# Reordering six items' steps in a hand-planned attention and MLP kernel: one transpose-back and one normalisation earlier, one score product ahead of a value product, two filler steps out

## The chip, the cores and the metric

The kernel runs on 1 core of one Trainium2 chip. The metric is the device time of one execution in microseconds. A core has five engines that each work through a list of their own in order: TensorE (PE, with its weight loads shown apart as PEld), VectorE (DVE), ScalarE (ACT), GpSimd (POOL) and SyncE (SP, which here only issues DMAs). They wait for one another by semaphores.

## The reference

Eight batches of twelve heads, 448 positions, 64 features, go through attention with normalised queries and keys; the result, seen as 3584 tokens of 768 features, goes through an MLP with a hard swish.

```python
q_n = q / (np.linalg.norm(q, axis=-1, keepdims=True) + 1e-06)
k_n = k / (np.linalg.norm(k, axis=-1, keepdims=True) + 1e-06)
scores = np.matmul(q_n, k_n.transpose(0, 1, 3, 2)) / tau
scores = scores - np.max(scores, axis=-1, keepdims=True)
attn = np.exp(scores)
attn = attn / (np.sum(attn, axis=-1, keepdims=True) + 1e-09)
out = np.matmul(attn, v)
...
h = x @ w_in                     # 768 -> 2048
g = h * np.clip(h + 3.0, 0.0, 6.0) / 6.0
return g @ w_out                 # 2048 -> 768
```

## The kernel before, in words

**Items.** The work of the attention is cut into 48 items, numbered from 0; an item is two heads of one batch (A and B), six items make a batch. Items 0 to 5 are batch 0, item 6 is the first of batch 1. The change calls them first, second and so on: the second item is number 1, the fourth 3, the fifth 4, the sixth 5, the seventh 6.

**An order written out by hand.** `PLAN` (lines 19 to 117) is a long list of steps such as `SC.5.3.1`. A loop at the end (line 1198) runs through it and calls for each step the function of that name with its numbers; each issues its instructions on its engine there and then. So the order of the list is the order of each engine's own list, and two steps on different engines only order each other where one needs the other's data or buffer. The framework puts the semaphore waits in. A letter at the end of a step names the engine (v for DVE, p for POOL, a for ACT).

**The steps of an item.** `LQ` and `LV` load queries, keys and values (SP, lines 254 to 281). `SQ`, `RE` and `NO` make the norms (any engine, DVE, ACT). `NM.j` scales a pair of items' queries or keys with them (line 333; j counts such pairs: items 6 and 7 are pairs 6 and 7). `TR.j` transposes them on PE into one of two PSUM banks, Y or Z (line 393), and copies bring the parts to SBUF: `CQ.i` the queries of item i (line 431), `CK.i` its keys (line 436), and from item 6 on `CS.i` the last 64 keys of either head, apart (line 450: for items 6 and 7 a memset and two small copies on DVE). `kz0` holds the keys of even items, `kz1` of odd ones.

`SC.i.g` makes the scores of item i on PE, keys along the partitions (line 474). Group g of 0, 1, 2 is a block of 128 keys of head A and one of head B, as two matmuls into two banks; group 3 is what is left of both, 64 keys each. `EX.i.g` takes exp on ACT, from PSUM to SBUF (line 508). No maximum is subtracted. `VA.i.g` multiplies the exps with the values on PE, 8 small matmuls of 65 columns for each block, all into the one accumulator PV (line 529); the 65th column is the sum of the exps. `VC.i` brings the values into bf16 (line 352).

`FI.i` is the normalisation of an item's result (line 548): a reciprocal of the sums and a multiplication, both on DVE, from PV to an SBUF tile `on`. PV is free for the next item's first `VA` once `FI` has read it. There are two buffers of `on`, and each holds two items: items 0 and 1, then 2 and 3, then 4 and 5 in the buffer of 0 and 1:

```python
        if i % 2 == 0:
            needs(("BK", i - 4), ("BK", i - 3))
            twin_on[i // 2] = sb.tile([128, 2, 4, 2, D], BF16, name="on", tag="on", bufs=2)
```

`BK.i` transposes an item's `on` on PE into a bank (four transposes, line 565), and `CX.i` copies it into `xT`, the input of the MLP (line 585). Later items go through a crossbar DMA instead (`XB`, `XP`; and `XD` in place of `TR`, line 404).

**Banks.** In the start-up phase, items 0 to 5, scores go to two tiles of two banks each (`SC0`, `SC1`; the last number of `SC.5.3.1` names the tile), and Y and Z serve the transposes. `OPEN` (line 1146) ends this phase: the four banks become M0 to M3, and from then on scores, transposes and MLP products take their banks in turn from one ring:

```python
        ring.extend([m[0], m[1], Y, Z, m[2], m[3]])
```

So `SC.6.0`, the first after `OPEN`, goes to M0 and M1, `SC.6.1` to Y and Z, `BK.4` to M2, `SC.6.2` to M3 and M0, and so on. With `startup.close()` the old tiles are given back, and the new ones wait for the readers of the old.

**Fillers.** `DP.n` issues n matmuls of 248 columns on zeros, into a part of PV that nobody reads (line 1139):

```python
            nc.tensor.matmul(
                PV[:, 0, 260:508], zeros[:, 0:128], zeros[:, 0:248], start=first, stop=first, skip_group_check=True
            )
```

**The MLP.** `F.b.n` is a 128-feature block of the first product (six matmuls of 448 columns, line 662), `FA` and `FV` its hard swish on ACT and DVE; `G`, `P`, `PE` and others make the second product with sums that save multiplications. From 39 us on these steps stand between those of the attention; the last two batches' first product follows the attention.

Of the kernel before, what the change touches and what calls it, by code (L numbers as in the profile page):

```python
# [23 lines left out]
    "TR.3.Y CK.2.v SC.1.3.1 DP.1 SC.2.0.0 SQ.6.a.0.7 VA.1.0 VA.1.2 EX.1.3 SC.2.1.1 NM.5.p RE.7 EX.2.0 EX.2.1 CK.3.v VA.1.3 RE.6 SQ.8.p.0.7 VA.1.1 SC.2.2.0",  # L24
    "FI.1 EX.2.2 SC.2.3.1 EX.2.3 TR.4.Y VA.2.0 NO.3 LV.2 CQ.3.v SC.3.0.0 CQ.4.v CQ.5.v VC.4.v VA.2.1 VA.2.2 VA.2.3 SC.3.1.1 FI.2 TR.5.Z EX.3.0 EX.3.1",
    "CK.4.v BK.0.Y LV.3 LQ.9 RE.8 SC.3.2.0 SC.3.3.1 VA.3.0 EX.3.2 SC.4.0.0 EX.3.3 EX.4.0 CK.5.v CX.0.v SQ.9.v.0.7 VA.3.2 SC.4.1.1 VA.3.1 SC.4.2.0 VA.3.3",
    "FI.3 BK.2.Z CX.2.v EX.4.1 EX.4.2 NM.6.p TR.6.Y SC.4.3.1 EX.4.3 SC.5.0.0 EX.5.0 VA.4.0 RE.9 W.3 W.1 VA.4.3 SC.5.1.1 VC.6.p VA.4.2 VA.4.1 CQ.7.v CQ.6.v",
    "SC.5.2.0 EX.5.1 EX.5.2 NM.7.p TR.7.Z CK.6.v VC.5.p LQ.10 BK.3.Y CX.3.v SQ.10.p.0.7 SC.5.3.1 CS.7.v EX.5.3 NO.4 BK.1.Y FI.4 DP.3 VA.5.0 CS.6.v OPEN",
    "VA.5.2 SC.6.0 CX.1.v CK.7.v NM.8.p EX.6.0 VA.5.3 VA.5.1 FI.5 SC.6.1 EX.6.1 BK.4 CX.4.v SC.6.2 SC.6.3 EX.6.2 EX.6.3 BK.5 CX.5.v VA.6.0 VA.6.1 TR.8",
    "CQ.8.v CQ.9.v LQ.11 SQ.11.p.0.7 SC.7.0 VA.6.2 EX.7.0 VA.6.3 SC.7.1 SC.7.2 F.0.2 EX.7.1 EX.7.2 RE.11 RE.10 SC.7.3 EX.7.3 FA.0.2 F.0.7 FA.0.7 FI.6",  # L30
    "NM.9.p TR.9 CK.9.v CK.8.v CS.8.v CS.9.v F.0.1 LQ.14 LQ.13 SQ.13.a.0.7 NO.5 F.0.3 FA.0.1 FV.0.7 FV.0.2 FV.0.1 VC.7.p W.5 FA.0.3 LQ.12 LV.4 SQ.12.p.0.7",
    "SC.8.0 SC.8.1 FV.0.3 RE.12 LV.5 W.4 VC.8.p VA.7.0 EX.8.0 EX.8.1 NM.10.p F.0.0 FA.0.0 SC.8.2 VA.7.3 FV.0.0 VA.7.1 VA.7.2 VC.11.p EX.8.2 SC.8.3 EX.8.3",
    "SC.9.0 EX.9.0 F.0.4 RE.13 FI.7 SC.9.1 NM.11.p VC.10.p FA.0.4 FV.0.4 SC.9.2 TR.10 VA.8.0 VA.8.1 EX.9.1 NO.6 NM.13.p SC.9.3 CQ.11.v TR.11 CQ.10.v",
    "CS.11.v EX.9.2 EX.9.3 CK.11.v LQ.15 VA.8.2 F.0.6 VA.8.3 CS.10.v CK.10.v SC.10.0 FA.0.6 FV.0.6 EX.10.0 F.0.5 FA.0.5 SC.10.1 SC.10.2 SC.10.3 FI.8 VC.9.p",
    "VA.9.0 VA.9.2 VA.9.1 EX.10.1 EX.10.2 EX.10.3 FV.0.5 VA.9.3 FI.9 SC.11.0 EX.11.0 F.0.10 FA.0.10 FV.0.10 SQ.14.a.0.7 NM.12.p W.9 VA.10.0 TR.12 CQ.13.v",
    "CQ.12.v VA.10.1 SC.11.1 VA.10.3 SC.11.2 XP.6 VA.10.2 FI.10 EX.11.1 EX.11.2 F.0.14 FA.0.14 BK.8 SC.11.3 EX.11.3 CX.8.a BK.9 VA.11.0 TR.13 VA.11.2 RE.14",
    "CS.12.a CX.9.v LV.6 FV.0.14 CK.12.v CS.13.a CK.13.v F.0.15 FA.0.15 VC.12.p SQ.15.p.0.7 FV.0.15 SC.12.0 SC.12.1 RE.15 EX.12.0 EX.12.1 VA.11.1 F.0.13",
    "SC.12.2 VA.11.3 FI.11 FA.0.13 FV.0.13 BK.10 CX.10.a NO.7 F.0.12 FA.0.12 EX.12.2 F.0.9 W.8 LQ.16 SQ.16.v.6.1 SQ.16.p.0.6 RE.16 VA.12.0 BK.11 CX.11.v",
    "NM.15.p NM.14.p FV.0.12 F.0.8 LQ.20 LQ.17 LQ.19 SQ.17.a.0.7 RE.17 FA.0.8 SC.12.3 FV.0.8 G.6.0.p FA.0.9 FV.0.9 F.1.4 FA.1.4 EX.12.3 FV.1.4 F.1.1 FA.1.1",
    "FV.1.1 SC.13.0 SC.13.1 SQ.19.v.0.7 RE.19 EX.13.0 EX.13.1 LQ.18 SQ.18.p.0.7 F.1.5 FA.1.5 FV.1.5 LV.7 XD.15 XD.14 W.7 W.6 F.1.9 FA.1.9 FV.1.9 F.0.11",  # L40
    "VA.12.3 VC.13.a WS.7.1 FA.0.11 FV.0.11 F.1.15 FA.1.15 F.1.6 G.1.0.p G.2.0.p FA.1.6 RE.18 FV.1.15 CS.14.v FV.1.6 NO.8 NM.16.p F.1.8 SC.13.2 CK.15.v",
    "VA.12.1 LQ.21 SQ.21.p.0.7 VC.15.p SC.13.3 VA.12.2 FA.1.8 FV.1.8 FI.12 VC.14.a F.1.0 NM.17.v WS.y4.1 EX.13.2 EX.13.3 NO.9 F.1.10 CK.14.v FA.1.10",
    "FV.1.10 FA.1.0 NM.18.p GL.0.p FV.1.0 F.1.11 FA.1.11 SC.14.0 FV.1.11 EX.14.0 F.1.12 FA.1.12 FV.1.12 SC.14.1 SC.14.2 F.1.3 SQ.20.a.0.7 FA.1.3 G.7.0.v",
    "EX.14.1 EX.14.2 VA.13.0 VA.13.3 VA.13.2 VA.13.1 FI.13 FV.1.3 F.1.7 FA.1.7 FV.1.7 XD.16 SC.14.3 SC.15.0 VA.14.0 VA.14.2 VA.14.1 EX.14.3 EX.15.0 XD.17",
    "WS.6 SC.15.1 SC.15.2 VA.14.3 SC.15.3 EX.15.1 EX.15.2 F.1.2 FA.1.2 CK.16.v SC.16.0 EX.15.3 FI.14 CK.17.v FV.1.2 WS.y3 EX.16.0 LV.8 VC.16.a F.1.13",
    "FA.1.13 XP.12 LV.9 VA.15.0 VA.15.2 VA.15.3 SC.16.1 EX.16.1 SC.16.2 VA.15.1 NM.19.p CS.16.v XD.18 XD.19 FV.1.13 FI.15 F.1.14 FA.1.14 VC.17.a SC.16.3",
    "P.3.1 FV.1.14 LQ.22 XP.14 EX.16.2 WS.7.0 WS.y4.0 LQ.23 VA.16.0 SC.17.0 VA.16.1 G.5.0.p P.3.0 LV.11 RE.21 EX.16.3 VA.16.3 G.7.1.v EX.17.0 PE.3.1.a",
    "SC.17.1 SC.17.2 VA.16.2 CK.18.v PE.3.0.a EX.17.1 FI.16 XB.16 EX.17.2 P.5.0 PE.5.0.a SC.17.3 VA.17.0 RE.20 WS.1 VA.17.1 EX.17.3 SC.18.0 SC.18.1 EX.18.0",
    "EX.18.1 SC.18.2 VA.17.3 VA.17.2 G.5.1.p P.4.0 P.5.1.a FI.17 XB.17 NO.10 NM.20.v PE.4.0.v CK.19.v CS.18.v XD.20 LQ.24 LQ.25 VC.18.a P.1.0 P.7.0 EX.18.2",
    "BO.0 LV.10 SQ.22.a.0.7 G.1.1.p P.2.0 PE.2.0.a PE.1.0.v PE.7.0.v RS.0 SC.18.3 VA.18.0 NM.21.p XD.21 P.6.0 RE.22 PE.6.0.v SQ.23.a.0.7 RE.23 G.6.1.v",  # L50
    "LQ.26 VA.18.1 SC.19.0 EX.18.3 PE.5.1.a EX.19.0 VA.18.2 F.2.2 FA.2.2 FV.2.2 SQ.24.v.0.7 SC.19.1 SC.19.2 EX.19.1 EX.19.2 VA.18.3 FI.18 CK.21.v CK.20.v",
    "F.2.3 F.2.12 NO.11 FA.2.12 G.2.1.p FA.2.3 FV.2.3 NM.22.p LQ.27 PL.5.1 SC.19.3 FV.2.12 CS.20.v P.4.1 EX.19.3 XD.22 VC.19.v LV.12 F.2.13 FA.2.13 FV.2.13",
    "P.2.1.a F.2.14 VA.19.0 VA.19.2 F.2.5 NM.23.p LQ.28 XD.23 PE.2.1.a PE.4.1.v PL.2.1 VC.21.p BO.1 RS.1 SQ.25.a.0.7 F.2.11 VC.20.p RE.24 RE.25 VA.19.1",
    "FA.2.14 FV.2.14 FA.2.5 SQ.26.a.0.7 FA.2.11 F.2.6 FV.2.5 FV.2.11 VA.19.3 SC.20.0 SC.20.1 FA.2.6 FV.2.6 P.1.1 PE.1.1.v FI.19 EX.20.0 EX.20.1 SC.20.2",
    "VC.22.a NO.12 SC.20.3 F.2.9 CK.22.v FA.2.9 FV.2.9 EX.20.2 EX.20.3 P.6.1 PE.6.1.v F.2.7 XP.18 FA.2.7 FV.2.7 VA.20.0 VA.20.3 RE.26 SC.21.0 SC.21.1",
    "NM.24.v P.7.1 EX.21.0 LQ.29 LV.13 SC.21.2 SC.21.3 G.7.2.p NM.25.p VC.23.p EX.21.1 EX.21.2 VA.20.2 VA.20.1 G.6.2.p G.2.2.v PE.7.1.v SQ.27.a.0.7 RE.27",
    "F.2.8 CK.23.v CS.22.v XD.24 LQ.30 P.3.2 SC.22.0 VC.24.a EX.21.3 FA.2.8 FI.20 SQ.28.v.0.7 FV.2.8 RE.28 G.5.2.p PE.3.2.a EX.22.0 SQ.29.v.0.7 F.2.15",
    "FA.2.15 FV.2.15 NO.13 VA.21.0 P.5.2 PE.5.2.a VA.21.1 P.4.2 VA.21.3 PE.4.2.a BO.2 SC.22.1 SC.22.2 EX.22.1 EX.22.2 VA.21.2 RE.29 FI.21 XD.25 P.2.2",
    "PE.2.2.a SC.22.3 G.1.2.v NM.26.v VA.22.0 VA.22.1 SC.23.0 EX.22.3 SC.23.1 SC.23.2 VA.22.3 EX.23.0 EX.23.1 VA.22.2 CK.25.v FI.22 F.2.1 FA.2.1 SC.23.3",
    "FV.2.1 CK.24.v P.1.2 VA.23.0 F.2.4 XP.20 CS.24.v SQ.30.p.0.7 XD.26 PE.1.2.v NO.14 EX.23.2 EX.23.3 RS.2 NM.27.v LQ.32 LQ.31 P.6.2 VA.23.2 FA.2.4 FV.2.4",  # L60
    "SC.24.0 VA.23.3 PE.6.2.v SC.24.1 XD.27 SC.24.2 VA.23.1 EX.24.0 FI.23 P.3.3 NM.28.p NM.29.p EX.24.1 EX.24.2 SC.24.3 EX.24.3 PE.3.3.a XB.23 XB.22 P.7.2",
    "PE.7.2.v VC.25.p LQ.33 VA.24.0 VA.24.2 SC.25.0 SC.25.1 VC.26.a EX.25.0 SC.25.2 EX.25.1 VA.24.3 VA.24.1 EX.25.2 FI.24 G.1.3.v RE.30 F.2.10 SC.25.3",
    "EX.25.3 FA.2.10 CK.26.v FV.2.10 CK.27.v CS.26.v F.2.0 FA.2.0 FV.2.0 P.4.3 PE.4.3.a VA.25.0 VA.25.1 SC.26.0 SC.26.1 SC.26.2 VA.25.3 EX.26.0 VA.25.2",
    "G.7.3.v G.5.3.v G.6.3.v FI.25 EX.26.1 EX.26.2 SQ.32.a.0.7 SQ.31.p.0.7 F.3.11 F.3.12 FA.3.12 FA.3.11 P.5.3.a SC.26.3 EX.26.3 PE.5.3.a RE.31 G.7.4.v",
    "F.3.15 SQ.33.a.0.7 FA.3.15 NO.15 FV.3.11 G.5.4.v FV.3.12 G.2.3.p P.2.3.a VA.26.0 VA.26.2 XD.29 SC.27.0 SC.27.1 XD.28 CK.28.v FV.3.15 PE.2.3.v VA.26.3",
    "SC.27.2 LV.14 XP.24 LQ.34 LV.15 EX.27.0 EX.27.1 VA.26.1 FI.26 RE.33 PL.5.3 GL.2.p VC.27.v EX.27.2 F.3.0 FA.3.0 FV.3.0 F.3.3 FA.3.3 FV.3.3 F.3.14 F.3.4",
    "SC.27.3 RE.32 FA.3.14 VC.29.a NM.30.p LV.16 LQ.35 P.1.3 VA.27.0 VA.27.2 VA.27.1 FV.3.14 PL.2.3 EX.27.3 VA.27.3 SC.28.0 FA.3.4 BO.3 PE.1.3.v FV.3.4",
# [1167 lines left out]
```

## Time and profile before

| | |
|---|---|
| device time, three runs | 397.3, 398.22, 397.3 us (median 397.3) |
| the profiled execution | 397.24 us, of which the span of the instructions 395.4 |
| PE busy | 384.2 us, 97% of the span, 3782 matmuls |
| DVE busy | 308.8 us, 78% |
| ACT busy | 295.3 us, 75% |
| POOL busy | 297.5 us, 75% |
| HBM read, written | 46.73 MB, 11.01 MB |
| chain that ended last | PE 87%, POOL 5%, DVE 2%, DMA 2% |

How to read the views that follow. In a timeline a row has the start in us from the span's beginning, the duration of the row in us, the engine, the line of the kernel, the operation, what it writes and from what, how many instructions are merged in the row, and in brackets how long the engine stood idle before it and whose end released it. Matmuls are pipelined: the duration of a row goes to the end of the last one, so rows overlap; the step from one row's start to the next is what PE's list needs. In the busy time by stretches each row has the stretch, its length, and for PE, PEld, DVE, ACT and POOL the busy us and the number of instructions, then the granted clock, the share of the DMA engines' time, and GB/s. In the list of waits the numbers are the us in total, the count and the longest. Tile names have their numbers left out: `SC` is SC0 or SC1, `M` any of M0 to M3, `kz` either key tile, `PV` the accumulator.

### The profile page before, as it was taken

How to read it: one execution, taken by the hardware profiler on the slowest of the kernel's cores; microseconds unless marked ns; L12 is line 12 of the kernel's file. 1: busy time of each engine (PE TensorE's matmuls, PEld its weight loads, DVE VectorE, ACT ScalarE, POOL GpSimd, SP SyncE). 2: the span in 40 equal slices, each digit the busy share in tenths (PEclk: the TensorE clock that was granted, in tenths of full speed). 3: DMA queues.
4: the chain of work that ended last, by engine and by line, in shares of the span. 5: the costliest groups of instructions: out<-in, count | busy, mean ns of one | idle time of the engine just before them, and what ended most of it. 6: DMA issues, size and time to landing. Idle time of an engine off the chain costs nothing.

```text
span 395.4 us, 10013 instructions
## 1 busy us (share of the span) xinstructions
PE 384.2 (97%) x3782; PEld 240.4 (61%) x3782; DVE 308.8 (78%) x545; ACT 295.3 (75%) x670; POOL 297.5 (75%) x269
## 2 busy tenths in 40 slices
PE   7898999999999999999999999999999999999995
PEld 5565556445655555655655556655566679977763
DVE  6998869988969697787767878853878968986862
ACT  6997999889966888887757876897787567744420
POOL 4999894899589947477848684778798988675752
PEclk9999999999999999999999999999999999999999
DMA  8989989798999797886995599665456350012124
GB/s 294 327 225 279 201 248 259 135 173 166 225 206 235 161 233 191 167 211 194 174 222 136 151 200 183 193 150 133 105 124 139 80 117 2 2 41 61 41 60 119
DMA packets 90239, 64.87 MB, mean 164 GB/s; under 512 B 55760, under 2 KB 89424, under 8 KB 90192
## 3 DMA queue, kind: packets, MB, share of 16 engines
q1 hardware_dynamic: 85280, 57.56, 59.1%
q0 software_dynamic: 4512, 6.29, 9.5%
q8 instruction: 29, 0.48, 0.5%
q10 hardware_dynamic: 400, 0.39, 0.3%
q14 instruction: 18, 0.15, 0.1%
HBM read 46.73 MB, written 11.01 MB: 146 GB/s over the span
## 4 chain that ended last, share of the span: by engine, by line
PE 87%; POOL 5%; DVE 2%; DMA 2%; issue 2%; ACT 1%; SPq 0%; POOLq 0%; DVEq 0%; ACTq 0%
PE M L671 18%; PE M L837 17%; PE PV L537 10%; PE V L837 6%; PE M L1026 6%; PE M L502 6%; PE Y L671 4%; PE Y L837 4%; PE Z L837 4%; PE Z L671 3%; POOL nrm L341 2%; PE Y L502 2%; PE Z L502 2%; POOL vx L363 1%; PE Y L1026 1%
## 5 line engine op out<-in xcount | busy, mean ns | idle before, releaser
L521 ACT ACTIVATE att<-M 128x448 bf16<-128x448 f32 x193 | 95.7, 561 | 13.9 <-PE M L502 12.2
L671 PE MATMUL M<-xT,w_in_sb 128*128 128x448 bf16 x396 | 82.9, 353 | 0.0
L671 PEld LDWEIGHTS <-w_in_sb 128*128 128x128 bf16 x576 | 53.1, 98 | 46.8 <-issue 3.4
L341 POOL TENSOR_TENSOR nrm<-big,r 128x896 bf16<-128x896 f32 (+1 forms) x36 | 61.7, 1720 | 15.0 <-ACT r L329 13.8
L537 PEld LDWEIGHTS <-att 128*128 128x128 bf16 (+1 forms) x1536 | 55.5, 97 | 23.0 <-issue 10.4
L537 PE MATMUL PV<-vx,att 128*128 128x65 bf16 (+1 forms) x1536 | 64.1, 193 | 0.5 <-POOL vx L363 0.5
L837 PEld LDWEIGHTS <-gT 128*128 128x128 bf16 x448 | 43.0, 98 | 27.7 <-issue 0.4
L686 DVE SCALAR_TENSOR_TENSOR gT<-u,M 128x448 bf16<-128x448 bf16 x66 | 39.5, 616 | 18.7 <-ACT u L680 18.4
L310 DVE TENSOR_REDUCE n<-big 128x14 f32<-128x896 f32 (+1 forms) x50 | 51.5, 1042 | 1.6 <-ACT big L296 1.3
L680 ACT ACTIVATE u<-M 128x448 bf16<-128x448 f32 x66 | 35.8, 555 | 10.8 <-PE M L671 9.7
L298 POOL TENSOR_TENSOR big<-big 128x896 f32<-128x896 f32 (+2 forms) x19 | 31.5, 1658 | 12.4 <-DMA big<-in_k_dram 6.9
L837 PE MATMUL M<-w_out_sb,gT 128*128 128x384 bf16 x224 | 40.4, 326 | 0.0
L837 PEld LDWEIGHTS <-gs 128*128 128x128 bf16 x296 | 28.1, 98 | 18.8 <-issue 1.3
L812 POOL TENSOR_TENSOR gT<-gT 128x1024 bf16<-128x1024 bf16 x15 | 31.9, 2125 | 9.5 <-DVE gs L812 9.0
L558 DVE TENSOR_TENSOR on<-PV,rc 128x512 bf16<-128x512 f32 x48 | 33.2, 691 | 1.6
L837 PE MATMUL M<-w_sum,gs 128*128 128x384 bf16 (+1 forms) x192 | 34.0, 323 | 0.0
L502 PE MATMUL M<-tT,kz 64*128 64x448 bf16 (+1 forms) x171 | 33.2, 354 | 0.6 <-DVE gT L686 0.4
L868 POOL TENSOR_TENSOR big<-big 128x384 f32<-128x384 f32 x14 | 18.3, 1308 | 17.7 <-ACT big L625 15.0
L812 POOL TENSOR_TENSOR gs<-gT 128x1024 bf16<-128x1024 bf16 x14 | 29.7, 2126 | 2.3 <-DVE gT L686 1.2
L521 ACT ACTIVATE att<-Z 128x448 bf16<-128x448 f32 x51 | 28.5, 559 | 1.3 <-PE M L502 1.0
L521 ACT ACTIVATE att<-Y 128x448 bf16<-128x448 f32 x50 | 28.0, 561 | 1.2 <-PE Z L502 1.2
L458 POOL COPY km<-tT 64x128 bf16<-64x128 bf16 x34 | 16.4, 483 | 12.5 <-PE Y L502 5.1
(146 smaller groups left out, 756.6 us busy)
## 6 DMA issues: line engine op xcount, KB each, us to landing
big<-in_q_dram SPq DMA_DIRECT2D x24, 448.0 KB, 4.4
big<-in_k_dram SPq DMA_DIRECT2D x24, 448.0 KB, 4.5
out_dram<-o SPq DMA_DIRECT2D x107, 96.0 KB, 2.2
big<-in_v_dram SPq DMA_DIRECT2D x68, 128.0 KB, 3.2
big<-in_v_dram SPq DMA_DIRECT2D x7, 448.0 KB, 7.6
w_out_sb<-in_moe_w_out_dram POOLq DMA_DIRECT2D x4, 768.0 KB, 10.2
w_in_sb<-in_moe_w_in_dram POOLq DMA_DIRECT2D x4, 384.0 KB, 5.8
w_in_sb<-in_moe_w_in_dram POOLq DMA_DIRECT2D x2, 768.0 KB, 8.3
```

The source lines that it names most:

```text
L298: engines[e].tensor_tensor(out=o, in0=i, in1=i, op=ALU.mult)
L310: nc.vector.tensor_reduce(out=n2s[d % 2][:, j % 2, c], in_=sq[:, :, :, :].rearrange("p g c d -> p (g c) d")[:, c, :], axis=AX.X, op=ALU.add,)
L341: engines[e].tensor_tensor(out=nrm[:, :, g, :].rearrange("p c g d -> p g c d"), in0=raw_of[j][:, g, :, :], in1=rs[d % 2][3][:, j % 2, :] . ...
L502: nc.tensor.matmul(o, ks, qt[rows], start=True, stop=True)
L521: nc.scalar.activation(out=o, in_=x, func=AF.Exp, scale=inv_tau)
L537: nc.tensor.matmul(pv_out(j, h), at[rows, n, q_cols(i // HP, j)], vt[rows, 3 + h if name == "M" else 5 * h + int(name[1]), :], start=(name ...
L558: nc.vector.tensor_tensor(out=on[:, :, :, :].rearrange("p j h d -> p h j d"), in0=pv4[:, :, :, 0:D], in1=rc[:, :, :].to_broadcast([128, 2, ...
L671: nc.tensor.matmul(ps[:, 0:S], w_in_sb[:, cc, fc * 128 : (fc + 1) * 128], x[:, cc, 0:S], start=(cc == 0), stop=(cc == CC - 1),)
L680: nc.scalar.activation(out=u[:, :], in_=ps[:, 0:S], func=AF.Relu, bias=0.5, scale=1.0 / 6.0)
L686: nc.vector.scalar_tensor_tensor(out=g[:, fc, c0 : c0 + S], in0=u[:, :], scalar=1.0, in1=ps[:, 0:S], op0=ALU.min, op1=ALU.mult,)
L812: engines[e].tensor_tensor(out=o[:, :, :], in0=x, in1=y, op=op)
L837: nc.tensor.matmul(m, lhs[:, c, :], rhs[:, c, c0 : c0 + width], start=(base is None and c == 0), stop=(c == KC - 1), skip_group_check=True,)
```

## The change

Only `PLAN` changes. The lines of the list are also filled anew, so that nearly all of them differ as text; by steps it is this (unchanged steps between are shown where they are passed):

```diff
  TR.3.Y CK.2.v SC.1.3.1
- DP.1
  SC.2.0.0
...
  SC.5.2.0 EX.5.1 EX.5.2 NM.7.p TR.7.Z CK.6.v VC.5.p LQ.10
- BK.3.Y CX.3.v
+ BK.1.Y CX.1.v
  SQ.10.p.0.7 SC.5.3.1
+ FI.4
  CS.7.v EX.5.3 NO.4
- BK.1.Y FI.4 DP.3
+ BK.3.Y OPEN SC.6.0
  VA.5.0 CS.6.v
- OPEN
  VA.5.2
- SC.6.0 CX.1.v
+ CX.3.v
  CK.7.v NM.8.p EX.6.0 VA.5.3 VA.5.1 FI.5 SC.6.1
```

For the engines this means: on PE, BK.1 and BK.3 change places around SC.5.3; SC.6.0 moves ahead of VA.5.0 and VA.5.2; the three matmuls of DP.3 and the one of DP.1 go. On DVE, CX.1 and CX.3 change places, and FI.4 moves ahead of CS.7. ACT, POOL and SP keep their lists. What is computed is the same.

92 rows, old and new, of the table PLAN are left out of this document.

## The prediction

> **What bounds the kernel now.** I read the page first, then the busy time by stretches, what the matmul engine (PE) waited for, and the timelines of PE, DVE and ACT around 31 to 36 us, the place of the change.
>
> ```profile
> span 395.4 us, 10013 instructions
> ```
>
> ```profile
> core 0: us, PE busy (x) PEld busy (x) DVE busy (x) ACT busy (x) POOL busy (x), PEclk, DMA share, GB/s
> 31.00:36.00 5.00, 3.35 (x56) 2.56 (x56) 3.32 (x14) 2.93 (x9) 4.81 (x6) 1.00 0.99 256
> 36.00:60.00 24.00, 23.61 (x297) 13.65 (x296) 18.75 (x43) 23.29 (x56) 21.62 (x24) 1.00 0.94 247
> 60.00:150.00 90.00, 89.76 (x852) 50.09 (x849) 78.78 (x124) 77.13 (x180) 68.59 (x51) 1.00 0.91 198
> 150.00:250.00 100.00, 99.91 (x962) 58.75 (x960) 76.03 (x129) 75.61 (x177) 70.36 (x58) 1.00 0.80 182
> ```
>
> From 36 us on PE is busy in 213.28 of 214 us up to 250, so it works through its list with hardly a hole; from 31 to 36 it is busy in 3.35 of 5. Its waits after 36 us are two:
>
> ```profile
> PE M L502 <- DVE gT L686: 0.4, 1, 0.4
> PE M L502 <- DVE kz L448: 0.2, 1, 0.2
> ```
>
> So time won or lost on PE's list before 36 us should come out at the end nearly whole, and no more than about 0.6 us of waiting is left behind that point to be won. The hole itself, on PE:
>
> ```profile
> 31.32 0.56 PE L398 MATMUL Z<-ident,nrm 128*128 128x128 bf16 x7 [0.32 <-POOL nrm L341]
> 31.72 0.39 PE L575 MATMUL Y<-ident,on 128*128 128x128 bf16 x4
> 32.03 0.38 PE L499 MATMUL SC<-tT,kz 64*64 64x448 bf16 x2
> 32.63 0.38 PE L575 MATMUL Y<-ident,on 128*128 128x128 bf16 x4 [0.22 <-DVE xT L420]
> 34.13 0.48 PE L1142 MATMUL PV<-xT 128*128 128x248 bf16 x3 [1.12 <-DVE on L558]
> 34.44 0.65 PE L537 MATMUL PV<-vx,att 128*128 128x65 bf16 x16
> 35.02 0.36 PE L502 MATMUL M<-tT,kz 64*128 64x448 bf16 x2
> 35.22 0.63 PE L537 MATMUL PV<-vx,att 64*128 64x65 bf16 x16
> 35.79 0.36 PE L502 MATMUL Y<-tT,kz 64*128 64x448 bf16 x1
> 35.79 0.36 PE L502 MATMUL Z<-tT,kz 64*128 64x448 bf16 x1
> ```
>
> In the plan's names these are TR.7, BK.3, SC.5.3, BK.1, DP.3, then VA.5.0 with VA.5.2, SC.6.0, VA.5.3 with VA.5.1, and SC.6.1 (two rows). PE stands for 1.12 us until FI.4 (L558) has read PV. DVE in the same stretch:
>
> ```profile
> 31.92 0.36 DVE L420 COPY kz<-Z 128x384 bf16<-128x384 bf16 x1 [0.84 <-PE Z L398]
> 32.19 0.38 DVE L420 COPY xT<-Y 128x448 bf16<-128x448 bf16 x1
> 32.64 0.09 DVE L463 MEMSET kz<- 64x32 uint32 x1
> 32.73 0.39 DVE L420 COPY kz<-Z 64x64 bf16<-64x64 bf16 x2
> 33.14 0.21 DVE L557 RECIPROCAL rc<-PV 128x8 f32<-128x8 f32 x1
> 33.38 0.69 DVE L558 TENSOR_TENSOR on<-PV,rc 128x512 bf16<-128x512 f32 x1
> 34.14 0.09 DVE L463 MEMSET kz<- 64x32 uint32 x1
> 34.23 0.39 DVE L420 COPY kz<-Z 64x64 bf16<-64x64 bf16 x2
> 34.66 0.39 DVE L420 COPY xT<-Y 128x448 bf16<-128x448 bf16 x1
> 34.97 0.35 DVE L420 COPY kz<-Z 128x384 bf16<-128x384 bf16 x1
> 35.90 0.21 DVE L557 RECIPROCAL rc<-PV 128x8 f32<-128x8 f32 x1 [0.58 <-PE PV L537]
> ```
>
> That is CK.6, CX.3, CS.7 (two rows), FI.4 (two rows), CS.6 (two rows), CX.1, CK.7, and FI.5. From 31.92 to 35.32 no row has a wait before it: DVE is the full engine of this stretch. And ACT:
>
> ```profile
> 32.51 0.54 ACT L521 ACTIVATE att<-SC 128x448 bf16<-128x448 f32 x1 [0.50 <-PE SC L499]
> ...
> 33.77 0.23 ACT L329 ACTIVATE r<-le 128x28 f32<-128x28 f32 x1
> 35.42 0.98 ACT L521 ACTIVATE att<-M 128x448 bf16<-128x448 f32 x2 [1.42 <-PE M L502]
> ...
> 36.29 0.55 ACT L521 ACTIVATE att<-Y 128x448 bf16<-128x448 f32 x1
> ```
>
> ACT has nothing from 34.00 to 35.42, since SC.6.0 stands behind VA.5.0 in PE's list.
>
> **The change, part by part.**
>
> *BK.1 before BK.3, each with its copy.* Both are four transposes into Y and one 0.38 copy on DVE, so PE's and DVE's amounts stay. What changes is whom they release: FI.4 writes the buffer that held items 0 and 1 (two buffers, three pairs of items), so it may not run before BK.1 has read it. BK.1 now stands in the place of the row at 31.72 and is done at 32.11; CX.1 runs at 32.19 to 32.57, BK.3 follows at 32.63. Cost nothing; should the swap be taken alone, FI.4 would still stand behind CS.7.
>
> *FI.4 before CS.7.* On DVE CS.7 takes 32.64 to 33.14, 0.50, and moves behind FI.4. FI.4 then starts at 32.64, and its end goes from 34.07 to 33.57. CS.7, CS.6, CX.3 and CK.7 follow: the same ten rows in another order, so CK.7 ends where it did, near 35.32. CS.7's and CS.6's targets are read first by SC.7.3 and SC.6.3, the latter behind 36.39 in PE's list, so their delay is hidden. Should CK.7 come out otherwise: not earlier than without the 0.03 to 0.06 gaps between rows (about 0.1 in all), not later than by one more such gap.
>
> *SC.6.0 before VA.5.0.* It needs CK.6 (done 32.28) and the banks of the start-up scores, whose last readers end at 32.01 or at 33.05 (32.51 + 0.54). BK.3 leaves PE at about 32.95. So SC.6.0 starts between 32.95 and 33.10, under the wait for FI.4, and costs the path nothing; without that cover it would cost its step of 0.20 (35.02 to 35.22). What is queued behind it on PE is VA.5.0, which cannot start before 33.62 anyway. EX.6.0 then starts on ACT at 34.00, right after the row of 33.77, in place of 35.42.
>
> *DP.3 out.* Its step was 34.13 to 34.44, 0.31, on the path. *DP.1 out*:
>
> ```profile
> 18.69 0.27 PE L1142 MATMUL PV<-xT 128*128 128x248 bf16 x1 [0.30 <-DVE on L558]
> ```
>
> ```profile
> 18.56 0.38 DVE L420 COPY kz<-Y 128x448 bf16<-128x448 bf16 x1
> ```
>
> The next on PE, SC.2.0, needs the copy that ends at 18.94, so DP.1 lay in a wait: I take nothing, bounds 0 and its step of 0.10 (a third of 0.31).
>
> *The sum on PE.* VA.5.0 starts at 33.57 + 0.05 = 33.62 (34.07 to 34.13 is the hand-over in the row), against 34.44. VA.5.0 with VA.5.2 and the step after take 0.58 (34.44 to 35.02), VA.5.3 with VA.5.1 0.57 (35.22 to 35.79), so PE is free for SC.6.1 at 34.77, which would be 1.02 ahead. But SC.6.1 writes Y and Z: Y waits for CX.3 (35.05), Z for CK.7 (35.32). **What is late next is CK.7**, so the Z half starts at 35.32 + 0.05 = 35.37 instead of 35.79. Gain **0.42 us**; the bounds are 1.02 (CK.7 does not hold it) and 0 (given back later).
>
> FI.5 can start behind CK.7 at 35.34 instead of 35.90, 0.56 ahead; ACT reaches EX.6.1 when its scores are there, at 35.73 at the latest against 36.29, again 0.56. Both are ahead of PE by a little more than PE is of itself, so neither takes the gain back at once. POOL's list holds no moved step. No DMA is moved; the loads already issued do not depend on these steps.
>
> The profiled execution took 397.24 us (395.4 of span and 1.8 around it); less 0.42 that is 396.8. The median of the runs shown, 397.3, stands 0.06 above it: **396.9**.
>
> **A rule against the change.** The matmuls removed (DP) only occupy PE, and the clock has two rates in this trace, seen on matmuls of this very form, first in a stretch at the start, then a little later:
>
> ```profile
> 2.50:7.50 5.00, 4.99 (x25) 3.68 (x26) 2.85 (x7) 2.97 (x9) 1.68 (x9) 1.00 1.03 387
> ```
>
> ```profile
> 9.20 1.43 PE L1142 MATMUL PV<-xT 128*128 128x248 bf16 x12
> ```
>
> At first 25 of them take 5.00 us, 0.20 each; then 12 take 1.43, that is (1.43 - 0.27) / 11 = 0.105 each. After that no such slow stretch shows, the 1.12 us wait included. In the new order PE's longest hole should be 34.77 to 35.37, 0.6, with matmuls at 33.1 in what was the long one. By rows alone the rate stays.
> The Trainium skill's "TensorE: Matmul & The Clock Gate" (Part 1: The HAM clock gate) says that about 3.4 us without activity halve the rate, and (Part 4: PE-mode transpose) that transposes do not count as such activity. By that rule the stretch without counted work, from SC.5.3 to the next real matmul, becomes shorter here than it was, although the DPs go; the trace agrees so far that 1.7 us of it (32.41 to 34.13) did no harm.
>
> **The rivals.**
>
> *Given back later.* 0.42 us are lost at the next point where PE depends on something that does not move with it. For it: the two waits above, and ACT busy 23.29 of 24 between 36 and 60. Against it: both waits end with DVE work that itself follows from PE's results a few us before, and ACT's own list starts 0.56 earlier. Time: 397.3.
>
> *More than that.* The lead of DVE and ACT also removes the later waits: 0.42 + 0.4 + 0.2 = 1.0, or PE keeps the 1.02. Time 396.3; with both, 397.3 - 1.6 = 395.7. Against it: CK.7 is at the end of a full DVE list, and the waits move along with PE.
>
> *A transfer falls out of step (slower).* The chain that ended last, and the landing times of all the crossbar transposes from SP's queue, which feed the scores from 70 us on:
>
> ```profile
> 151.94 2.89 DMA tT<-nrm
> ```
>
> ```profile
> DMA to landing us min/median/max: 2.9/3.5/5.7
> ```
>
> The chain passes through one of these transposes. That one landed as quickly as any. With loads and stores shifted by half a us against each other, it may take the longest, 5.7: 2.8 later, less 0.42, is 399.7; it decides against the change from a landing of 3.3 on, at the median of 3.5 it already makes 397.5. For it: the DMA queues are 80 to 90% busy there. Against it: stores, loads and transposes are issued in one order from one queue, and what triggers them moves together.
>
> *The clock falls at 33 us (slower).* As long as at the start, at least 5.0 us at half rate, loses 2.5: 397.3 - 0.4 + 2.5 = 399.4. It decides as soon as a hole halves the rate for 0.84 us. Against it: the paragraph on the clock.
>
> **How the numbers follow.** Forecast 396.9: 0.5, its own range 396.5 to 397.2. Given back: 0.12, at 397.3. More: 0.18, at 395.7 to 396.3, two thirds of it below 396.1. Transfer: 0.16, from 397.5 to 399.7, half of it above 398.5. Clock: 0.04. About 0.3%, 1.2 us, is what a measurement of this kernel can tell from no change; so faster is below 396.1 (0.12) and slower above 398.5 (0.12). A single run also stood at 398.22 where two others stood at 397.3, on either side of the comparison, so I add 0.1 to faster, where the forecast lies nearer, and 0.04 to slower: faster 0.22, within 0.62, slower 0.16. The range of 8 in 10 leaves out the far ends of the two slower cases and the best of the better one: 395.9 to 398.5.
>
> **What would show it.** In the profile after: no DP in 32 to 35; FI.4's multiplication ending near 33.57; SC.6.0 near 33.0 and EX.6.0 at 34.0; VA.5.0 at 33.6; a wait of PE of about 0.6 before SC.6.1, ended by DVE's kz copy, and SC.6.1 at 35.37; FI.5 at 35.3. Then every PE group later ahead of its old place by 0.4, at 100 as at 300 us. A lead at 36 us that is smaller at 60, 150 or 250 speaks for a give-back and tells where; a lead that grows, for the third case; matmuls of 248 or 448 columns at twice their spacing, for the clock. The prediction is wrong in its core if SC.6.1 starts later than 35.7 or before 35.1.

## The result, and the profile after

| | before | after |
|---|---|---|
| median of 20 runs each, one comparison | 397.87 us (397.22 to 399.48) | 396.68 us (396.56 to 398.16) |
| the profiled execution | 397.24 us | 398.16 us |
| TR.7 to the last PE group in the profile | 357.22 us | 356.51 us |

The ratio is 0.9968, with a 95% interval of 0.9958 to 0.9978. The two lowest runs are 0.66 us apart, the two medians 1.19. Why these differ is taken up in the part on the clock, below.

The profiled execution of the changed kernel is the longest of its 20 runs, so its absolute times say little. The page of the profile and ACT's timeline show where it differs; the second view has the row of before first, then that of after (start, duration, and in brackets the idle time before the row and its releaser):

```profile
span 396.3 us, 10005 instructions
```

```profile
6.79 0.94 ACT L296 ACTIVATE big<-big 128x896 f32<-128x896 f32 x1
```

```profile
8.62 0.95 ACT L296 ACTIVATE big<-big 128x896 f32<-128x896 f32 x1 [1.62 <-DMA big<-in_q_dram]
```

ACT stood 1.62 us for a load of queries, at a point where it has no such wait in the profile of before. TR.7 starts at 32.94 in place of 31.32, 1.62 later. The first step that the change touches is DP.1, at 18.7 us, so this is a late load and not the change. I therefore compare inside each profile: from the start of TR.7 (row `Z<-ident,nrm` x7) to the start of the last PE group, and call the difference to before the **lead**. The last group in PE's timeline, before and then after:

```profile
388.54 2.76 PE L837 MATMUL V<-w_sum,big 128*128 128x384 bf16 x16
```

```profile
389.45 2.76 PE L837 MATMUL V<-w_sum,big 128*128 128x384 bf16 x16
```

388.54 - 31.32 is 357.22, 389.45 - 32.94 is 356.51: a lead of 0.71 us. PE's timeline of the kernel after, where the prediction showed that of before:

```profile
32.94 0.56 PE L398 MATMUL Z<-ident,nrm 128*128 128x128 bf16 x7 [0.21 <-POOL nrm L341]
33.34 0.39 PE L575 MATMUL Y<-ident,on 128*128 128x128 bf16 x4
33.66 0.38 PE L499 MATMUL SC<-tT,kz 64*64 64x448 bf16 x2
34.25 0.38 PE L575 MATMUL Y<-ident,on 128*128 128x128 bf16 x4 [0.22 <-DVE xT L420]
34.56 0.36 PE L502 MATMUL M<-tT,kz 64*128 64x448 bf16 x2
35.09 1.24 PE L537 MATMUL PV<-vx,att 128*128 128x65 bf16 x32 [0.17 <-DVE on L558]
36.51 0.35 PE L502 MATMUL Y<-tT,kz 64*128 64x448 bf16 x1 [0.18 <-DVE xT L420]
36.77 0.35 PE L502 MATMUL Z<-tT,kz 64*128 64x448 bf16 x1
```

Counted from TR.7, SC.6.0 now starts at 1.62 (34.56 - 32.94), under the wait for FI.4, whose rest is 0.17. VA.5.0 starts at 2.15 instead of 3.12 (34.44 - 31.32), 0.97 earlier. SC.6.1's two halves no longer start together: Y's at 3.57 waits for an `xT` copy, Z's at 3.83 instead of 4.47. So 0.64 of the 0.97 is left when both halves have gone. DVE in the same stretch shows who holds them:

```profile
33.54 0.36 DVE L420 COPY kz<-Z 128x384 bf16<-128x384 bf16 x1 [0.83 <-PE Z L398]
33.81 0.38 DVE L420 COPY xT<-Y 128x448 bf16<-128x448 bf16 x1
34.11 0.20 DVE L557 RECIPROCAL rc<-PV 128x8 f32<-128x8 f32 x1
34.35 0.69 DVE L558 TENSOR_TENSOR on<-PV,rc 128x512 bf16<-128x512 f32 x1
35.10 0.09 DVE L463 MEMSET kz<- 64x32 uint32 x1
35.20 0.39 DVE L420 COPY kz<-Z 64x64 bf16<-64x64 bf16 x2
35.55 0.09 DVE L463 MEMSET kz<- 64x32 uint32 x1
35.64 0.39 DVE L420 COPY kz<-Z 64x64 bf16<-64x64 bf16 x2
36.06 0.39 DVE L420 COPY xT<-Y 128x448 bf16<-128x448 bf16 x1
36.37 0.35 DVE L420 COPY kz<-Z 128x384 bf16<-128x384 bf16 x1
36.64 0.20 DVE L557 RECIPROCAL rc<-PV 128x8 f32<-128x8 f32 x1
```

CX.3 (36.06 to 36.45) lets the Y half go at 36.51, CK.7 (36.37 to 36.72) the Z half at 36.77. DVE is again full from CK.6 to CK.7. From there on PE has as few holes as before; first the busy time by stretches, then its list of waits from 36 us on:

```profile
36.00:60.00 24.00, 23.43 (x286) 13.43 (x288) 18.59 (x43) 22.65 (x56) 22.36 (x23) 1.00 0.96 257
60.00:150.00 90.00, 89.76 (x867) 50.19 (x866) 78.71 (x122) 77.14 (x180) 69.36 (x52) 1.00 0.94 199
150.00:250.00 100.00, 99.92 (x949) 58.56 (x946) 76.08 (x131) 76.26 (x178) 69.67 (x58) 1.00 0.81 182
```

```profile
PE M L502 <- DVE gT L686: 0.4, 1, 0.4
PE M L502 <- DVE kz L448: 0.2, 1, 0.2
PE Y L502 <- DVE xT L420: 0.2, 1, 0.2
```

The two later waits have the size that they had, and only the wait of SC.6.1 is new. The lead taken at single PE groups is 0.67 at 38 us, 0.68 at 60 and 100, 0.69 from 150 to 250 and 0.71 at the end: it is made between 32 and 38 us and carried whole. The last 0.04 do not come again in the second profile of after, whose lead at the end is 0.65.

### The profile page after: what moved, and what is told of

Read it like the earlier page. It is cut to its first block, busy times and chain, and to the rows that moved or that the text cites. A ratio compares the mean times of both kernels' runs of the same rounds, so it can differ in the third digit from the quotient of the medians.

```text
span 396.3 us, 10005 instructions
## 1 busy us (share of the span) xinstructions
PE 382.6 (97%) x3778; PEld 239.3 (60%) x3778; DVE 308.5 (78%) x545; ACT 295.4 (75%) x670; POOL 297.2 (75%) x269
## 4 chain that ended last, share of the span: by engine, by line
PE 86%; ACT 4%; DVE 3%; DMA 2%; POOL 2%; issue 1%; SPq 0%; POOLq 0%; DVEq 0%; ACTq 0%
PE M L671 18%; PE M L837 17%; PE PV L537 10%; PE V L837 6%; PE M L1026 6%; PE M L502 6%; PE Y L671 4%; PE Y L837 4%; PE Z L837 4%; PE Z L671 3%; ACT att L521 2%; DMA big<-in_q_dram 2%; PE Y L502 2%; PE Z L502 2%; PE Y L1026 1%
## 5 line engine op out<-in xcount | busy, mean ns | idle before, releaser
L686 DVE SCALAR_TENSOR_TENSOR gT<-u,M 128x448 bf16<-128x448 bf16 x66 | 39.5, 616 | 18.7 <-ACT u L680 18.4
```

The source lines that it names most:

```text
L686: nc.vector.scalar_tensor_tensor(out=g[:, fc, c0 : c0 + S], in0=u[:, :], scalar=1.0, in1=ps[:, 0:S], op0=ALU.min, op1=ALU.mult,)
```

## The experiments

All edits are in the plan, by steps as in the change above; `+` and `-` stand against the kernel named. The table has the runs of each kernel; the before of the same comparisons stood at medians of 397.52 to 397.77. Each lead is that of one profile, and a ratio's interval is that of the runs.

| kernel | runs | median, lowest us | ratio to before, 95% | lead us |
|---|---|---|---|---|
| before again | 12 | 397.83, 397.32 | 1.0007 [0.9992, 1.0023] | -0.03 |
| after again | 12 | 396.76, 396.63 | 0.9971 [0.9961, 0.9982] | 0.65 |
| before without DP.1 | 12 | 397.49, 397.22 | 0.9992 [0.9974, 1.001] | 0.02 |
| before without DP.3 | 12 | 397.16, 396.88 | 0.9983 [0.9969, 0.9998] | 0.31 |
| before, BK/CX exchanged and FI.4 forward | 11 | 396.82, 396.6 | 0.997 [0.9952, 0.9988] | 0.70 |
| before, SC.6.0 forward | 11 | 397.5, 397.04 | 0.9987 [0.9974, 0.9999] | 0.22 |
| before, FI.4 behind CK.7 | 6 | 400.36, 398.39 | 1.0069 [1.0044, 1.0093] | -2.35 |
| after, ring in another order | 7 | 396.52, 396.42 | 0.9975 [0.9958, 0.9991] | 0.93 |
| before, matmuls on zeros in the gap | 11 | 397.56, 397.32 | 1.0001 [0.9984, 1.0018] | 0.05 |
| before, FI.4 forward alone | 12 | 396.82, 396.64 | 0.9985 [0.9971, 0.9998] | 0.10 |
| before, a second profile | 1 | 398.89 | | -1.37 |
| before, a third profile | 1 | 397.29 | | 0.03 |

**The two kernels again.** Both as they were, to see how far leads and medians repeat.

> The kernel before, unchanged, timed against itself: this shows how far medians of one and the same program stand apart. Theory A (the reorder at 31 to 36 us gives all of the change's gain, about 0.7, and the rest of the measured 1.2 is scatter of the first 15 us, which hits any program): ratio within 0.9985 to 1.0015, the lowest time near 397.2, single runs up to 399, and from TR.7 to SC.6.1 4.48 us as in the profile of before. Theory B (the kernel before has disturbed starts more often than the one after, and that is worth 0.5 in the median): its median is again 0.5 or more above its lowest time.

> The changed kernel once more. Theory A: lowest time 0.65 to 0.75 below the lowest of before, near 396.55; from TR.7 to SC.6.1 3.84 us; its share of disturbed runs (0.4 or more above the lowest) like that of before in the same session, so that the medians differ by 0.7 too. Theory B: few disturbed runs while before has many, medians 1.0 or more apart.

The leads repeat to 0.06 us (-0.03; 0.65 against 0.71). Nothing of the 1.62 us at the start is seen in this second profile of after, where TR.7 starts at 31.62. So the late load was an event of one execution. The medians are 1.07 apart, as theory B has it: the 12 runs of after all lie between 396.63 and 396.89, while 5 of the 12 of before stand above 398.7. B also puts the disturbance at the start; the profile below that catches one of before has it at 34.6 us.

**The fillers, each out alone.**

```diff
- DP.1
```

> Before with the filler DP.1 at 18.7 us taken out, nothing else. Theory A: the wait for CK.2's copy stays, so 0.0 (ratio 0.9985 to 1.0015, lowest time near 397.2), TR.7 to SC.6.1 4.48. Theory B in the form that DP.1 makes the starts worse: median 0.4 or more below that of before. A rival on the path: DP.1's step of 0.10 is won.

The lead begins at TR.7, behind DP.1, and cannot show it. PE's timeline of this kernel at the place itself does:

```profile
19.19 0.36 PE L502 MATMUL SC<-tT,kz 64*128 64x448 bf16 x2 [0.61 <-DVE kz L420]
```

SC.2.0 starts 0.98 after SC.1.3 (18.21 to 19.19), as in before (18.02 to 19.00), and now waits for the key copy itself: DP.1 is worth nothing, it lay in that wait.

```diff
- DP.3
```

> Before with the filler DP.3 at 34.1 us taken out, nothing else. VA.5.0 then follows FI.4 directly and all up to SC.6.1 moves by 0.31; CK.7 ends at 35.31 and lets SC.6.1 go at 35.36, before 35.48, so the whole 0.31 is won: from TR.7 to SC.6.1 4.17, time 0.3 below before. Rival (the clock falls without the filler): slower by 1 us or more, with matmuls of 448 columns further apart than 0.19 after 33 us. Rival (given back later): the lead of 0.31 is gone at 60 or 150 us.

VA.5.0 in PE's timeline of this kernel, whose TR.7 starts at 31.52:

```profile
34.34 0.66 PE L537 MATMUL PV<-vx,att 128*128 128x65 bf16 x16 [1.12 <-DVE on L558]
```

It starts 2.82 after TR.7 instead of 3.12, and the lead at the end is 0.31: DP.3 costs its whole step, when nothing else holds SC.6.1.

**FI.4 forward with the exchange of BK and CX, DP.3 and SC.6.0 left as in before.**

```diff
- BK.3.Y CX.3.v
+ BK.1.Y CX.1.v
  SQ.10 SC.5.3.1
+ FI.4
  CS.7.v EX.5.3 NO.4
- BK.1.Y FI.4
+ BK.3.Y
  DP.3 VA.5.0 CS.6.v OPEN VA.5.2 SC.6.0
- CX.1.v
+ CX.3.v
  CK.7.v
```

> Of the change only the two transposes-back exchanged with their copies, and FI.4 ahead of CS.7; SC.6.0 stays behind VA.5.2, DP.3 and DP.1 stay. By the lists of the profile after, seen from TR.7: VA.5.0 about 0.65 earlier than before, DP.3 still in front of it, SC.6.1 free on PE at the moment at which CK.7 is done: TR.7 to SC.6.1 3.85, so the whole 0.65 of the change without SC.6.0's move. Rival (SC.6.0's move carries the gain): about 0.1 to 0.2 only. Theory C (in some runs of before the clock falls for one stretch, because PE has almost only transposes and waiting between 31 and 34.4 us; this is what sets the medians further apart than 0.7): runs with a mean granted clock of 0.994 to 0.996, 12 of 47 of before so far, become rare, since VA.5.0 ends the stretch 0.65 earlier.

In PE's timeline of this kernel (TR.7 at 31.62):

```profile
33.77 0.48 PE L1142 MATMUL PV<-xT 128*128 128x248 bf16 x3 [0.46 <-DVE on L558]
34.08 0.65 PE L537 MATMUL PV<-vx,att 128*128 128x65 bf16 x16
...
35.45 0.35 PE L502 MATMUL Z<-tT,kz 64*128 64x448 bf16 x1
```

VA.5.0 is 0.31 later than in after (2.46 against 2.15), because DP.3 is still there, and yet the Z half of SC.6.1 starts 3.83 after TR.7, as in after. The lead of 0.70 is the whole of the change's. Taking out DP.3 and moving SC.6.0 therefore add nothing in the new order; what they save on PE ends in the wait for CK.7.

**SC.6.0 forward alone**, FI.4 where it was.

```diff
  BK.1.Y
+ OPEN SC.6.0
  FI.4 DP.3 VA.5.0 CS.6.v
- OPEN
  VA.5.2
- SC.6.0
  CX.1.v
```

> Of the change only SC.6.0 ahead of VA.5.0 (the start-up banks given back earlier); the transposes-back, FI.4 behind CS.7, DP.1 and DP.3 as before. Main theory (DVE's order decides): FI.4 ends where it did, VA.5.0 starts where it did, and SC.6.1 wins only SC.6.0's own step, 0.2: TR.7 to SC.6.1 4.28. Rival (SC.6.0's move carries the gain through ACT): 0.5 or more. Theory C: its two matmuls near 33.0 us lie in the empty stretch, so runs of low clock become rarer than 12 of 47.

PE's timeline (TR.7 at 31.63):

```profile
33.25 0.36 PE L502 MATMUL M<-tT,kz 64*128 64x448 bf16 x2
34.44 0.48 PE L1142 MATMUL PV<-xT 128*128 128x248 bf16 x3 [0.82 <-DVE on L558]
34.75 1.23 PE L537 MATMUL PV<-vx,att 128*128 128x65 bf16 x32
```

VA.5.0 starts at 3.12, as in before, with SC.6.0 already done under the wait. The lead of 0.22 is SC.6.0's own step of 0.20, taken off the path.

**FI.4 last of DVE's stretch**: the suspected cause doubled in the other direction.

```diff
  BK.1.Y
- FI.4 DP.3 VA.5.0
  CS.6.v
- OPEN VA.5.2 SC.6.0
  CX.1.v CK.7.v
+ FI.4 DP.3 VA.5.0 OPEN VA.5.2 SC.6.0
  NM.8.p
```

> The opposite of the change: before, with FI.4 put behind CS.6, CX.1 and CK.7 on DVE as well, all else as it was. VA.5.0 then starts about 1.3 us later, near 35.7, and PE's stretch of transposes and waiting grows from 3.4 to 4.7 us. Main theory: TR.7 to SC.6.1 about 5.7 (1.2 to 1.3 later), carried to the end: lowest time near 398.5. Theory C: runs of low granted clock rise from a quarter to a half or more, each about 1.5 us longer again, and a profile that catches one shows the granted clock at half near 34 us. Without theory C (disturbed runs are scatter of the first loads): no more low clocks than in before.

PE's timeline, then its busy time by stretches with the granted clock behind the five engines:

```profile
35.32 0.53 PE L1142 MATMUL PV<-xT 128*128 128x248 bf16 x3 [2.14 <-DVE on L558]
```

```profile
32.20:35.60 3.40, 1.04 (x11) 0.72 (x10) 2.89 (x12) 1.34 (x5) 3.32 (x3) 1.00 0.92 246
35.60:39.00 3.40, 3.40 (x44) 2.35 (x42) 0.90 (x2) 1.46 (x4) 3.40 (x3) 0.50 1.01 362
```

PE's wait grew from 1.12 to 2.14, by 1.02, but the kernel lost 2.35. In the 3.4 us that follow, the clock was granted at one half. The other 1.33 is about what such a stretch costs by itself (1.37, in a profile of before below), and the one run of the six at a full clock, 398.39, stands 1.13 above the lowest of before. This raised the question whether the same happens in before, at its 1.12 us.

**Before, profiled twice more.**

> The kernel before, unchanged, for its profile alone. Theory C: with a chance of about one in four the profile shows the granted clock at half for one stretch of 3.4 us that begins near 34.4 us, and all after it 1.4 to 1.7 later; otherwise 4.48 from TR.7 to SC.6.1 as before.

> The kernel before once more, for its profile alone, with the same two outcomes: a stretch of 3.4 us at half clock near 34.4 us and 1.4 to 1.7 us lost (one in four), or none.

One of the two shows it. Its stretches (the third figure from the end is the granted clock), then its PE timeline:

```profile
31.20:34.60 3.40, 1.76 (x21) 1.26 (x20) 2.35 (x10) 2.44 (x7) 3.21 (x5) 1.00 1.06 218
34.60:38.00 3.40, 3.40 (x43) 2.39 (x41) 1.68 (x6) 1.26 (x3) 3.40 (x4) 0.50 0.95 312
38.00:41.40 3.40, 3.40 (x58) 2.12 (x56) 2.90 (x6) 3.26 (x8) 3.29 (x4) 1.00 0.98 362
```

```profile
34.85 1.09 PE L537 MATMUL PV<-vx,att 128*128 128x65 bf16 x16
35.87 0.56 PE L502 MATMUL M<-tT,kz 64*128 64x448 bf16 x2
```

VA.5.0 with VA.5.2 takes a step of 1.02 (34.85 to 35.87) for the 0.58 of the first profile of before. Nothing waits; PE is simply granted half its clock from 34.6 to 38.0, and 1.37 us are lost at the end. The other profile is like the first, with a lead of 0.03.

**The gap filled with matmuls on zeros**, the order of before unchanged.

```diff
  BK.1.Y
+ DS.4
  FI.4 DP.3
```

```python
nc.tensor.matmul(SC[0][:, 0, :], zeros[:, 0:128], zeros[:, :], start=True, stop=True)
```

> Before, with four matmuls of 512 columns on zeros added behind BK.1, into a start-up score bank whose readers are done: 4 times 0.21 lies in PE's wait for FI.4 (33.0 to 34.1), so the order and the steps stay: lead over before 0.0, lowest time as before's, near 397.25. Theory C (the clock falls because the stretch holds almost nothing but transposes and waiting): real matmuls in the stretch keep the clock, no run at a mean clock of 0.996 or less where before has 20 of 72, and the median comes down to within 0.3 of the lowest time, 0.2 to 0.5 under before's. Without theory C: low clocks as often as in before, 2 to 4 of 12.

`DS.4` issues that line four times. None of the 11 runs shows a fallen clock, and the lead of 0.05 says that the filling itself costs nothing. The median did not come down with it, against my expectation: it is 397.56 beside 397.52. Three of the runs stand at 398.87, 399.04 and 399.8 with a full clock, for which no run shows the cause. So no gain of the filling is shown in the time.

**FI.4 forward alone**, BK.3 before BK.1 as in before, to see whether the exchange was needed.

```diff
  SQ.10 SC.5.3.1
- CS.7.v EX.5.3 NO.4
  BK.1.Y FI.4
+ CS.7.v EX.5.3 NO.4
  DP.3 VA.5.0
```

> Before with FI.4 ahead of CS.7 but without the exchange of the transposes-back: FI.4 then has to wait for BK.1, which PE ends at 33.0 after CX.3, and DVE stands from 32.6 to 33.04. FI.4 gains 0.1, CK.7 ends 0.3 later, near 35.6: TR.7 to SC.6.1 about 4.35 to 4.40, lead 0.1. If instead the exchange is not needed: lead 0.65 as in the changed kernel. Theory C: low clocks nearly as often as in before.

FI.4 in DVE's timeline, then BK.1 and the next on PE:

```profile
32.61 0.20 DVE L557 RECIPROCAL rc<-PV 128x8 f32<-128x8 f32 x1
32.85 0.69 DVE L558 TENSOR_TENSOR on<-PV,rc 128x512 bf16<-128x512 f32 x1
```

```profile
32.75 0.38 PE L575 MATMUL Y<-ident,on 128*128 128x128 bf16 x4 [0.22 <-DVE xT L420]
33.59 0.48 PE L1142 MATMUL PV<-xT 128*128 128x248 bf16 x3 [0.46 <-DVE on L558]
```

FI.4 starts writing at 32.85, while BK.1 reads from 32.75 to 33.13: it did not wait for it. The lead is 0.68 up to 205 us, as large as with the exchange. At the end only 0.10 is left, and the chain that ended last shows where the rest went:

```profile
197.93 6.09 DMA big<-in_k_dram
...
210.40 2.14 POOL gT L812
...
212.58 1.48 PE M L837 x8
```

A load of keys took 6.09 us, where half of such loads in the same profile landed within 4.6 by its list of DMA issues (the last column):

```profile
big<-in_k_dram SPq DMA_DIRECT2D x24, 448.0 KB, 4.6
```

POOL's steps followed late, PE waited for them until 212.58, and the lead fell by 0.58, from 0.68 to 0.10. That is again one execution: the median of the 12 runs, 396.82, is that of the variant with the exchange.

**After, with the ring begun by all four M banks**, so that SC.6.1 need not wait for CX.3 and CK.7.

```diff
- ring.extend([m[0], m[1], Y, Z, m[2], m[3]])
+ ring.extend([m[0], m[1], m[2], m[3], Y, Z])
```

> The changed kernel with the ring's banks in another order, M0 M1 M2 M3 Y Z in place of M0 M1 Y Z M2 M3, so that SC.6.1 takes M2 and M3 and need not wait for CX.3 and CK.7 to empty Y and Z. If CK.7 is what comes late after the change, as predicted, PE goes on at 3.4 instead of 3.84 after TR.7, and with FI.5 next on DVE some 0.3 to 0.5 more are won in all: lead over before 1.0 to 1.2, lowest time near 396.2. Rival (something else, ACT or FI.5, is as late as CK.7): lead 0.65 to 0.75 as in the changed kernel.

PE's timeline (TR.7 at 31.44), then FI.5's multiplication on DVE:

```profile
34.77 0.36 PE L502 MATMUL M<-tT,kz 64*128 64x448 bf16 x2
35.06 0.37 PE L577 MATMUL Y<-ident,on 128*128 128x128 bf16 x4
...
35.37 0.66 PE L502 MATMUL M<-tT,kz 64*128 64x448 bf16 x2
36.12 0.37 PE L577 MATMUL M<-ident,on 128*128 128x128 bf16 x4
```

```profile
35.37 0.69 DVE L558 TENSOR_TENSOR on<-PV,rc 128x512 bf16<-128x512 f32 x1
```

SC.6.1 now goes to M2 and M3 at 34.77, 3.33 after TR.7, 1.14 ahead of before. Next late is BK.5 (36.12), which needs FI.5's result; FI.5 stands behind CK.7 on DVE and ends at 36.06 (35.37 + 0.69). The lead settles at 0.93, a little under the 1.0 to 1.2 expected. The median of 396.52 is the lowest of all kernels here; the interval of its ratio, 0.9958 to 0.9991, holds that of after, so by the runs alone it isn't told apart from after, by the lead it is 0.2 to 0.3 better.

## Why the prediction was right, and where it was off

**Direction, place and mechanism: right.** The gain comes from FI.4 ahead of CS.7 on DVE; CK.7 takes over as what holds SC.6.1; the lead is carried from 38 us to the end. The forecast was 396.9, measured is 396.68, and no trace of the two kernels shows a give-back, a removal of the two later waits or a transpose out of step. That the time came so near owes something to its base: 397.3 was the median of three runs of before, the 20 runs have 397.87, so the medians differ by 1.19 and not by 0.4.

**The fillers and SC.6.0: right.** DP.1 is worth nothing, DP.3 0.31 alone and nothing once FI.4 is early; SC.6.0 goes under the wait for FI.4 and costs nothing.

**Gain 0.42: too small by 0.22 us, and the step that failed is one term.** The prediction said of DVE "the same ten rows in another order, so CK.7 ends where it did, near 35.32", with at most about 0.1 from the gaps. From the start of CK.6 to the end of CK.7 it was 3.40 before (31.92 to 35.32) and is 3.18 after (33.54 to 36.72). The rows have the same durations to 0.01, but the step from one to the next depends on the neighbour. CX and then a memset: 0.45 (32.19 to 32.64). CX and then the reciprocal: 0.30 (33.81 to 34.11), which is less than the row's own 0.38. The two key copies and then the reciprocal: 0.41 (32.73 to 33.14); and then a memset: 0.35 (35.20 to 35.55). The two pairs make 0.15 + 0.06 = 0.21 of the 0.22. A wait of the first memset for SC.5.3, which last read its target, is not the reason: that ends at 32.41 (32.03 + 0.38), the copy before the memset at 32.57, and the second memset of before, whose target a product last read until 28.87 (SC.4.3, 28.49 + 0.38), starts as long behind its neighbour (34.07 to 34.14) as the first (32.57 to 32.64). What the rows do share is where they start. The memset (line 463) and the second of the two small copies work on partitions from 64 on, all the other rows from 0 on. Where the start is that of the row before, the next row begins 0.04 to 0.09 before that row's end; where it changes between 0 and 64, it begins up to 0.07 behind it. The old order has eight such changes and the new one six: CX and the reciprocal now follow each other, and so do the second small copy and a memset. Only the multiplication of `FI` does not fit by itself, but it needs the reciprocal's result. This holds for all the rows of both orders shown; no run tests it alone. The hold by CK.7 was right, its time was not: 0.42 + 0.22 is the 0.64 seen on SC.6.1. By the times of before its Z half starts at 35.15 (31.32 + 3.83), just inside the 35.1 that the prediction named as the sign of being wrong. The rows of before already showed such an overlap (CK.6's copy has a row of 0.36 and a step of 0.27), so a sum over steps with their neighbours, rather than over rows, would have been possible.

**BK.1 ahead of FI.4 for the buffer's sake: wrong, without a price.** "FI.4 may not run before BK.1 has read it" is what the `needs` line suggests, but it only orders the steps as they are issued. A half of the buffer belongs to each item, and item 4 writes item 0's half. The run with FI.4 forward alone shows FI.4 writing while BK.1 still reads. The exchange was not needed for the gain.

**The clock: the rival had the wrong sign.** It was expected, at 0.04, to fall in the kernel after. It falls in the kernel before, in some executions, and the change takes that away. Of the 97 runs of before in the experiments, whose mean granted clock is recorded, 27 stand at 0.996 or less; of 32 runs of after none does, nor does any of the 52 of the other kernels with FI.4 or SC.6.0 forward, the other ring or the filled gap. With DP.1 or DP.3 out alone, where the gap is as long as in before, it is 1 of 12 each. With FI.4 late it is 5 of 6, three of them at 0.991. By estimate, one stretch of 3.41 us at half rate takes 0.5 x 3.41 / 396 = 0.0043 off the mean, which stands at 0.997 to 1 in the profiles without a fall; so 0.993 to 0.996 fits one such stretch and 0.991 two. Only two falls were profiled, one in before and one with FI.4 late.

The prediction took one profile without a fall as a sign that the 1.12 us did no harm. More than a quarter of the runs would have said otherwise, and of the three times shown of before the 398.22 perhaps was one of them. Among the 95 runs of before in the comparisons of the experiments, 69 at a higher clock have a median of 397.44 and 26 at a lower one 398.99. So at a full clock the change is worth 397.44 - 396.71 (the median of the 32 runs of after), 0.73 us, which is the lead. The falls add 26/95 x 1.55, about 0.4 us, to the mean of before; 0.7 and 0.4 make 1.1, and the interval of the ratio (0.22% to 0.42% of 397.87) is 0.9 to 1.7 us. For the 20 runs of before in the first comparison no clocks are recorded, so that their share of falls is open.

The traces also show why only some runs fall. Their records of the granted clock put the rise at the start (where the spacing of the fillers goes from 0.207 to 0.106 us) and the fall at 7.28 and 34.59 us in the second profile of before, at 8.31 and 35.62 with FI.4 late. Both times 27.31 us lie between, eight times 3.41. Counted on in such steps from the rise, the emptiest stretch around the gap had PE busy for 1.77 and 1.05 us of 3.41 in these two, and for 2.08, 1.91, 2.08, 2.11 and 2.29 in the five profiles of the old order of FI.4 and SC.6.0 without a fall and without the filling (before three times, DP.1 out, DP.3 out). The one nearest to a fall, before again:

```profile
31.34:34.75 3.41, 1.91 (x24) 1.48 (x25) 2.42 (x10) 2.20 (x7) 3.22 (x5) 1.00 1.01 211
```

In the profiles with FI.4 or SC.6.0 forward, the other ring or the filled gap, PE is busy for at least 2.05 us wherever between 30 and 39.9 us a stretch of 3.41 is laid. So where the steps of 3.41 happen to lie against the gap decides, with a bound between 1.77 and 1.91 us of busy PE, transposes counted. These are seven profiles, not a proof: with the steps laid at random, about 18 positions in 100 would be under 1.91, fewer than 27 of 97. The granted clock printed for 2.50 to 7.50 us in the prediction is 1.00 although the spacing there is double, so for the start the spacing counts.

The Trainium skill's "TensorE: Matmul & The Clock Gate" (Part 1: The HAM clock gate) describes a free-running window of about 3.4 us after which the rate is set to one half or the whole. The half-rate stretch of 34.6 to 38.0 is as long as that, and that it falls in some runs of the same kernel fits a window that isn't tied to the program's start. Its summary warns of idle gaps of more than about 3 us; here PE's longest idle time before the fall was 1.11, so for this kernel the warning comes too late.

**Scatter.** A difference of 0.7 us is as small as what one late load does: 1.62 us in the profile of after, 0.58 in that of FI.4 forward alone. Of the 69 runs of before at a higher clock, 15 still stand above 397.9. The lead inside one profile repeated to 0.06.

## What to carry to other kernels

When an accumulator holds up the next product, put the normalisation that frees it ahead of copies that are read later, and then look for what is late next, since the copy at the end of that list takes over most of the rest. Sum an engine's list by steps from row to row with their actual neighbours, and compare two kernels by the distance between two fixed instructions in one profile before trusting medians that a late load can move as much. A stretch of a few us that holds little but transposes and waits, right before dense matmuls, is worth shortening even if no single profile shows a loss there: look at the clock of many runs. Filling it kept the clock here, but no gain in time was measured.

## What was not expected of the hardware

- **The matmul clock fell without a long idle time.** In the second profile of before, PE was busy in 1.76 of the 3.40 us from 31.2 to 34.6, mostly with transposes, and waited 1.11 at a time; the next 3.4 us ran at 0.50, at a cost of 1.37 us. With four matmuls on zeros in the gap none of 11 runs fell; at the share of 27 in 97 that would come by chance in about 3 of 100 cases, (70/97) to the power of 11. That alone is weak, since the two kernels with one filler out, which leave the gap as it was, fell in only 2 of 24. The 84 runs of after and of the kernels with less of a gap, none of which fell, weigh more. Whether the transposes count as activity no run here separates.
- **Steps on VectorE depend on the pair.** A copy of 0.38 lets a reciprocal start after 0.30 and a memset after 0.45; the ten rows in their new order take 0.22 us less. In the rows of both kernels a row overlaps the one before it only where it starts at the same partition, 0 or 64.
